# Scores in gate/up's array shape, from a zero-interleaved K ring, in a sliding-window attention and gated-MLP kernel

## The chip, the cores and the metric

The kernel runs on one core of one Trainium2 chip, as one program. The core has five engines with a queue each: TensorE (PE in the profile; its weight loads are listed as PEld) for matrix products, VectorE (DVE), ScalarE (ACT), GpSimd (POOL), and SyncE (SP), which issues the DMAs here. The engines meet at semaphores. PSUM, where PE writes, has eight banks of 512 float32 columns on 128 partitions; SBUF holds everything else. The metric is the device time of the program in microseconds (us). Three runs of the kernel before took 564.13 to 564.35 us, median 564.28.

## The reference

One sequence of 2048 tokens, 576 features. A layer norm without weights feeds two branches, and the output is x + attention x silu(MLP).

```python
xn = _layernorm(x, axis=-1)
# branch A: 32 heads of 18 features, causal window of 256 tokens
qkv = (xn @ wqkv)                               # 576 x 1728
scores = jnp.einsum("bhqd,bhkd->bhqk", q, k) * (18 ** -0.5)
mask = (idx[:, None] - idx[None, :] >= 0) & (idx[:, None] - idx[None, :] < 256)
p = _softmax(jnp.where(mask[None, None], scores, -1e9), axis=-1)
s = einsum("bhqk,bhkd->bhqd", p, v) -> (tokens, 576) @ wo
# branch B: 4608 hidden features
h = _sigmoid(xn @ w_gate) * (xn @ w_up)
g = _silu(h @ w_down)
return x + s * g
```

All inputs and the output are bfloat16.

## The kernel before

The tokens are cut into four chunks of 512 queries (`c` = 0 to 3). For each chunk the builder makes operations for the layer norm (L441 applies it), the Q, K and V projections (`project`, L491), attention, the output projection wo (L800), gate and up (`build_ffn`, L879), down (called f2, L1006) and the final product. The operations of all chunks go to a planner, `schedule`, a list scheduler with a cost for each operation (`mm_ns`, `act_ns`, `dve_ns`), a priority, and an extra cost `MODE_NS` of 94 ns where PE goes from one `mode` to another. It fixes the order of instructions on each of the five queues; on the chip each queue runs in that order and waits at semaphores. So attention of a chunk is woven into the gate/up matmuls of the same chunk.

The features are cut into 9 blocks of 64. Gate/up works in mode "r64": a matmul has 64 rows (half of the array) and 128 columns, and two of them, one on rows 0 to 63 and one on rows 64 to 127, run at the same time. A gate tile and an up tile have 9 such matmuls of 512 columns each; there are 36 hidden tiles to a chunk. ACT takes the gate's tanh (L893), DVE multiplies with up (L897, `hm`), and this frees the two banks. Gate/up uses banks 4 to 7. Projections and wo are r64 as well, with 288 columns. Down is mode "full" (128 x 128).

Heads stand in groups of four, `hg` = 0 to 7, each head in a strip of 32 partitions of `qkp`, the transposed Q and K (made by transposing DMAs from `pk`). Two head groups make a pair. A score unit (`build_unit`, mode "r32", L637) computes keys x queries in eight small tiles at once: four heads on four row strips of 18 rows, times two column halves of 64 keys, `low` the even key blocks of 64 and `up` the odd ones. Its pieces are runs of 1 to 6 query blocks of 64 columns. It fills all of banks 0 to 3, two exponentials of 128 x 1024 on ACT (L655) read them into `expr` (a ring of five), and DVE multiplies masks in (L673). The first chunk has two units per head group; the others have five per pair, as the blocks of the chunk before are needed as well: their K is kept by a tail copy on POOL (L684) which runs after the group's scores.

After a pair's units comes PV (`build_pv`, mode "c32", L707): eight tiles of 64 keys x 32 columns (18 of V and a one for the denominator). The even and the odd key blocks lie on different partition halves, so they end in different banks: two banks for each head group, four for the pair. In the chunks after the first, DVE transposes both (L726, L728) and adds them (L731); in the first chunk, ACT copies one (L740), DVE adds (L742) and transposes (L747). Then come reciprocal (L754), scaling (L758) and the transpose back (L764), and DMAs scatter the result to `oT` for wo. `SC_GATE` = 0 holds a chunk's scores back until the first gate/up step of that chunk has been planned. V is evicted by one ACT copy for each 128 tokens (L582), Q by DVE (L545) and K by ACT (L546).

At the start, ten matmuls on ones (L365) keep PE busy until the first normalized tokens arrive.

## Time and profile before

| | |
|---|---|
| median of three runs | 564.28 us |
| profiled execution | 564.0 us, of which the span of the profile 561.8 us |
| PE busy | 556.6 us |
| DVE / ACT / POOL busy | 305.3 / 279.3 / 29.6 us |
| gate/up windows of the four chunks | 21.85 to 103.79, 157.21 to 242.07, 295.31 to 380.42, 433.65 to 518.68 us |
| exponentials (L655) | 152 of 1.023 us |
| masks (L673) | 152, of 0.42 us where they have 512 elements |
| score matmuls (L637), PV matmuls (L707) | 1472, 1440 |

The span is the time from the first to the last instruction; what lies around it (2.2 us) belongs to the measured time. A group's line gives the line of the code, engine and operation, what is written from what with the shape, the number, then the busy time and the mean length of one in ns, and the idle time before them. The chain is followed back from the last instruction to what released it each time; in order of time, each of its pieces has start, length, and how many instructions the trace shows of it.

### The profile page before, as it was taken

What the parts mean: (1) busy time and instruction counts of PE and PEld (TensorE: products, weight loads), DVE (VectorE), ACT (ScalarE), POOL (GpSimd) and SP (SyncE); (2) the same over time, 40 slices, a digit from 0 to 9 for tenths busy, and PEclk for the clock granted to TensorE, in tenths of its full rate; (3) what the DMA queues carried; (4) which work ended last, traced back from release to release, by engine and by line L of the source; (5) the groups of instructions that cost most, each with busy time, mean ns of one, the idle gap of its engine ahead of it and who ended that gap; (6) DMA issues with size and microseconds to landing.
All of it is one profiled execution on the core that took longest, in us unless ns stands there. A gap on an engine that the chain in (4) does not pass through costs nothing.

```text
span 561.8 us, 17998 instructions
## 1 busy us (share of the span) xinstructions
PE 556.6 (99%) x7890; PEld 290.3 (52%) x7890; DVE 305.3 (54%) x656; ACT 279.3 (50%) x382; POOL 29.6 (5%) x55
## 2 busy tenths in 40 slices
PE   8999999999999999999999999999999999999997
PEld 5754444558544444456754444445664444444554
DVE  6135998722147886671215778766211586776312
ACT  7438777314065856811407576580230856856021
POOL 3000110100000110010000011001000000000100
PEclk9999999999999999999999999999999999999999
DMA  8999889837925766135992665604587355650010
GB/s 202 220 201 233 185 199 224 207 80 141 232 60 132 160 140 153 40 56 88 148 214 75 147 152 132 145 26 75 88 169 173 77 128 128 149 130 25 20 43 21
DMA packets 125898, 73.29 MB, mean 130 GB/s; under 512 B 54654, under 2 KB 125310, under 8 KB 125822
## 3 DMA queue, kind: packets, MB, share of 16 engines
q1 hardware_dynamic: 125822, 72.16, 60.3%
q8 instruction: 62, 1.02, 0.8%
q14 instruction: 14, 0.11, 0.1%
HBM read 55.48 MB, written 2.36 MB: 103 GB/s over the span
## 4 chain that ended last, share of the span: by engine, by line
PE 98%; DVE 1%; DMA 0%; issue 0%; ACT 0%
PE ps L879 51%; PE ps L1006 24%; PE ps L491 9%; PE ps L637 5%; PE ps L707 3%; PE ps L800 3%; PE ps L1037 2%; DMA xr<-in_A_x_dram 0%; DVE bnst L428 0%; DVE bnst L430 0%; DVE xnr L441 0%; PE ps L465 0%; DVE hT L897 0%; DVE op__63 L764 0%; DVE pk L728 0%; DVE mv L432 0%
## 5 line engine op out<-in xcount | busy, mean ns | idle before, releaser
L879 PE MATMUL ps<-xn,wgs 64*128 64x512 bf16 x2522 | 290.2, 377 | 0.0
L879 PEld LDWEIGHTS ps<-xn,wgs 64*128 64x128 bf16 x2522 | 117.5, 94 | 138.6 <-issue 10.2
L655 ACT ACTIVATE expr<-ps 128x1024 bf16<-128x1024 f32 x152 | 149.3, 1023 | 23.4 <-PE ps L637 23.4
L1006 PE MATMUL ps<-wd_sb,hT 128*128 128x512 bf16 (+1 forms) x1080 | 133.7, 286 | 0.0
L897 DVE SCALAR_TENSOR_TENSOR hT<-tring,ps 128x512 bf16<-128x512 bf16 x144 | 98.2, 682 | 49.2 <-ACT tring L893 25.9
L893 ACT ACTIVATE tring<-ps 128x512 bf16<-128x512 f32 x144 | 86.2, 599 | 77.5 <-PE ps L879 58.3
L1006 PEld LDWEIGHTS ps<-wd_sb,hT 128*128 128x128 bf16 x1080 | 68.1, 98 | 65.1 <-issue 1.4
L1068 ACT ACTIVATE thf<-ps 128x576 bf16<-128x576 f32 (+2 forms) x17 | 10.6, 623 | 133.2 <-PE ps L1006 125.6
L673 DVE TENSOR_TENSOR expr<-expr,m 128x512 bf16<-128x512 bf16 (+2 forms) x152 | 58.2, 412 | 33.1 <-ACT expr L655 32.0
L1070 DVE SCALAR_TENSOR_TENSOR thf<-thf,ps 128x576 bf16<-128x576 bf16 (+2 forms) x17 | 12.2, 719 | 107.4 <-ACT thf L1068 107.3
L491 PE MATMUL ps<-wqkv_sb,xn 64*128 64x288 bf16 x864 | 55.1, 283 | 0.1
L491 PEld LDWEIGHTS ps<-wqkv_sb,xn 64*128 64x128 bf16 x864 | 44.5, 94 | 8.6 <-issue 0.6
L637 PEld LDWEIGHTS ps<-qkp 18*64 18x64 bf16 x1472 | 16.4, 103 | 32.9 <-ACT expr L655 19.1
L637 PE MATMUL ps<-qkp 18*64 18x320 bf16 (+4 forms) x1472 | 32.4, 259 | 0.1
L684 POOL COPY qkp<-qkp 128x256 bf16<-128x256 bf16 x24 | 10.2, 423 | 292.2 <-PE ps L637 292.2
L764 DVE STREAM_TRANSPOSE op__63<-pk 128x512 bf16<-128x512 bf16 x32 | 22.5, 702 | 0.2
L707 PEld LDWEIGHTS ps<-expr,vau 64*32 64x32 bf16 x1440 | 17.9, 92 | 7.2 <-issue 5.5
L707 PE MATMUL ps<-expr,vau 64*32 64x320 bf16 (+5 forms) x1440 | 20.7, 253 | 0.0
L1072 DVE TENSOR_TENSOR thf<-thf,sat 128x576 bf16<-128x576 bf16 (+2 forms) x17 | 7.5, 440 | 23.1 <-ACT sat L824 22.8
L800 PE MATMUL ps<-wo_sb,oT 64*128 64x288 bf16 x288 | 18.8, 283 | 0.0
L800 PEld LDWEIGHTS ps<-wo_sb,oT 64*128 64x128 bf16 x288 | 14.5, 94 | 3.5 <-issue 0.5
L728 DVE STREAM_TRANSPOSE pk<-ps 128x512 f32<-128x512 f32 x24 | 16.1, 670 | 0.0
(62 smaller groups left out, 220.8 us busy)
## 6 DMA issues: line engine op xcount, KB each, us to landing
wgs<-in_B_w_gate_dram SPq DMA_DIRECT2D x47, 240.0 KB, 3.8
wgs<-in_B_w_up_dram SPq DMA_DIRECT2D x47, 240.0 KB, 4.9
wgs<-in_B_w_up_dram SPq DMA_DIRECT2D x47, 192.0 KB, 4.0
wgs<-in_B_w_gate_dram SPq DMA_DIRECT2D x47, 192.0 KB, 4.6
wd_sb<-in_B_w_down_dram SPq DMA_DIRECT2D x9, 576.0 KB, 6.7
xf<-in_A_x_dram SPq DMA_DIRECT2D x18, 144.0 KB, 2.4
out_dram<-xf SPq DMA_DIRECT2D x15, 144.0 KB, 2.0
xr<-in_A_x_dram SPq DMA_DIRECT2D x14, 144.0 KB, 4.0
```

The lines of the kernel that those rows point to most:

```text
L491: r = e.matmul(self.bank(ps, HV, hf), self.xn[r0:r0 + 64, k, i * P:(i + 1) * P], self.wqkv_sb[r0:r0 + 64, j, k, :], start=(k == 0), stop=( ...
L637: r = e.matmul(self.ps[64 * half:64 * half + 64, b:b + n * 64], self.qkp[r0:r0 + DH, hg, k0:k0 + 64], self.qkp[r0:r0 + DH, hg, q0 * 64:(q0 ...
L655: return e.activation(self.expr[:, es, 2 * pr:2 * pr + 2, :], src, ACTF.Exp, scale=SM_SCALE)
L673: return e.tensor_tensor(ap, ap, m, ALU.mult)
L707: r = e.matmul(self.ps[32 * j:32 * j + 32, b + q0 * 64:b + (q0 + n) * 64], vf[:, v0:v0 + 32], self.expr[p0:p0 + 64, es, j, pos * 64:(pos + ...
L728: t3 = self.rd("DVE", dve_ns(CH), lambda e, tg=tg, hg=hg: e.transpose(tg, self.bank(ps2[hg][1])), f"t3:{c}:{hg}", deps=[o, self.last_mul] ...
L764: t2 = self.op("DVE", dve_ns(CH), lambda e, on=on: e.transpose(self.op_[:, hg % NOT, :], on.rearrange("p g d -> p (g d)")), f"t2:{c}:{hg}" ...
L800: r = e.matmul(self.bank(ps2[w], HV, n), self.oT[r0:r0 + 64, kt, qi * P:(qi + 1) * P], self.wo_sb[r0:r0 + 64, kt, n * HV:(n + 1) * HV], st ...
L879: return e.matmul(self.bank((pg, pu)[gu][ft]), w, self.xn[r0:r0 + 64, i, :], start=first, stop=last, tile_position=(r0, 0))
L893: return e.activation(self.tring[:, st_, :], self.bank(ps), ACTF.Tanh, scale=0.5)
L897: return e.scalar_tensor_tensor(self.hT[:, ft, :], self.tring[:, st_, :], 1.0, self.bank(ps), ALU.add, ALU.mult)
L1006: r = e.matmul(self.ps[:, b + n0:b + n1], lhsT, self.wd_sb[:, q, fl, n0:n1], start=(ft == 0), stop=(ft == NFT - 1))
```

## The change

- **Heads.** Head h and head h + 16 stand on the two strips of 32 partitions of one row half. A head group is now two such pairs of heads, one on each row half.
- **K ring.** `build_kd` is new. For each head group DVE writes K of four key blocks into a ring `kd` of four slots: for each block of 64 keys, 128 columns, of which the first 64 have the second head's rows multiplied by zero and the last 64 the first head's rows (`hm` holds the zeros and ones). Two multiplies fill a slot; the first chunk takes two slots per head group, the others three.
- **Scores.** With these weights a matmul has 64 rows and 128 columns, mode "r64". The keys of the one head come out on partitions 0 to 63 and those of the other on 64 to 127, one bank per row half. A unit holds eight blocks of 64 queries (six in one of the first chunk's) in two banks, (0, 1) or (2, 3), and has one exponential. There are four units per head group in the first chunk and five in the others. `expr` becomes ten slots of half the size. The gate `SC_GATE` is gone.
- **V** is kept twice in the row sense: partitions 0 to 63 hold the values of heads 0 to 15, 64 to 127 those of heads 16 to 31, for each half of 64 tokens. Its eviction is four instructions, two on ACT and two on DVE.
- **PV** sums all key blocks of a head in one bank: two banks for a pair. One DVE transpose per head group follows, with no addition; the first chunk's path by copies is gone.
- **Around it.** The first chunk's Q and K evictions are split between ACT and DVE; wo's rows are loaded in the new order of heads, by four DMAs in place of two (the eight small ones stay); the tail copy waits for `kd` in place of the scores; the tanh buffer `thf` of the final product is taken from `expr`'s ring; the warm-up has 22 matmuls of 16 columns and nine of 512; the masks are built slightly differently.

```diff
-NEXP = 5
+NEXP = 10
...
-RTH = 2
 RREC = 2
+RKD = 4
+KD_NS = 180.0
+SC_PRIO = 1
+KD_PRIO = 0
...
-SC_GATE = 0
...
-WARM = 10
+WARM = 9
+TINY = 22
...
-        self.vau = sb("vau", [P, NVB, H + 1, DH + 1], bf16)
-        self.expr = sb("expr", [P, NEXP, 4, CH], bf16)
...
+        self.vau = sb("vau", [P, NVB, 2, H // 2 + 1, DH + 1], bf16)
+        self.kd = sb("kd", [P, RKD, 4, 2, 64], bf16)
+        self.expr = sb("expr", [P, NEXP, 2, CH], bf16)
...
-        self.thf = sb("thf", [P, RTH, D], bf16)
...
         def f(e):
-            for k in range(n):
-                r = e.matmul(self.bank(ps), self.hT[:, 0, 0:P], self.hT[:, 0, :], start=True, stop=True)
+            for w in [16] * TINY + [512] * n:
+                r = e.matmul(self.bank(ps, w), self.hT[:, 0, 0:P], self.hT[:, 0, 0:w], start=True, stop=True)
             return r
-        self.op_warm = self.pe(n * WARM_NS, f, name, deps=deps, prio=-9, psum=[ps])
+        self.op_warm = self.pe(n * WARM_NS + TINY * 30, f, name, deps=deps, prio=-9, psum=[ps])
...
+        rows = self.wo.rearrange("(s h t p) c -> p h t s c", s=2, h=2, t=2, p=KL)
         n = KL - (P - KL)
+        self.op_wo = []
+        for h, (r0, k) in enumerate(((0, KL), (KL, P - KL))):
+            for t in range(2):
+                self.op_wo.append(self.dma(self.wo_sb[r0:r0 + k, 2 * t:2 * t + 2, :], rows[0:k, h, t, :, :], 2 * k * D * 2,
+                                           f"wo{h}{t}", ("wo", h, t), deps=gate, prio=6))
...
+        ev = []
+        for k, (part, act) in enumerate(((slice(0, 1), 1), (slice(1, 2), 0)) if c == 0 else ((slice(0, 2), j),)):
+            n = D // 2 if c == 0 else D
+            ev.append(self.rd("ACT" if act else "DVE", act_ns(n) if act else dve_ns(n),
+                              lambda e, part=part, act=act: f_ev(e, part, act), f"qke:{c}:{i}:{j}:{k}", deps=deps, prio=1,
+                              psum=[ps]))
...
-        self.op_v[st] = self.rd("ACT", act_ns(D), f_ve, f"ve:{st}", deps=[o, self.op_vones], prio=1, psum=[ps])
+        self.op_v[st] = []
+        for s_, eng in ((0, "ACT"), (1, "DVE")):
+            for p in range(2):
+                def f_ve(e, s_=s_, p=p):
+                    src = self.bank(ps, HV, s_)[64 * p:64 * p + 64, :].rearrange("p (h d) -> p h d", d=DH)
+                    dst = self.vau[64 * s_:64 * s_ + 64, vs, p, 0:H // 2, 0:DH]
+                    return e.activation(dst, src, ACTF.Copy) if s_ == 0 else e.tensor_copy(dst, src)
+                self.op_v[st].append(self.rd(eng, (act_ns if s_ == 0 else dve_ns)(HV), f_ve, f"ve:{st}:{s_}{p}",
+                                             deps=[o, self.op_vones], prio=1, psum=[ps]))
...
     def attn_steps(self, c):
-        steps = []
+        if c == 0:
+            units = ([(0, 0, 5, 0), (5, 5, 3, 5)], [(1, 1, 5, 0), (6, 6, 2, 5), (7, 7, 1, 7)],
+                     [(2, 2, 5, 0), (3, 3, 3, 5)], [(3, 6, 2, 0), (4, 4, 4, 2)])
+        else:
+            units = ([(0, 0, 5, 0), (-2, 0, 3, 5)], [(1, 1, 5, 0), (-3, 0, 2, 5), (-4, 0, 1, 7)],
+                     [(-1, 0, 4, 0), (4, 4, 4, 4)], [(2, 2, 5, 0), (6, 6, 2, 5), (7, 7, 1, 7)],
+                     [(3, 3, 5, 0), (5, 5, 3, 5)])
+        masks = ([(0, 4, 0), (5, None, 0)], [(0, 4, 0), (5, 7, (0,))], [(0, 4, 0), (5, None, 0)], [(1, 2, 1)]) if c == 0 \
+            else ([(0, 4, 0), (7, None, 1)], [(0, 4, 0), (6, 7, (1,))], [(3, 4, 1)], [(0, 4, 0), (5, 7, (0,))],
+                  [(0, 4, 0), (5, None, 0)])
+        return list(zip(units, masks))
+
+    def build_attn(self, c):
+        self.masks, self.runs = {}, {}
+        steps = self.attn_steps(c)
         for a in range(0, NHG, 2):
...
+            for hg in (a, a + 1):
+                self.build_kd(c, hg)
+                for u, (pieces, masks) in enumerate(steps):
+                    self.build_unit(c, hg, u, pieces, masks)
+                for s_ in self.slots_kd.values():
+                    for o in self.op_sc[c][hg]:
+                        self.r_kd.release(s_, o)
+            self.build_pv(c, a)
+
+    def build_kd(self, c, hg):
+        self.slots_kd, self.ops_kd = {}, {}
+        for g in range(1 if c == 0 else 0, 3):
+            s_, ds = self.r_kd.take()
+            self.slots_kd[g] = s_
+            self.ops_kd[g] = []
+            deps = ds + self.op_hm + (([self.op_tail[hg]] if g == 0 else self.op_k[2 * g - 2:2 * g]))
+            for half in range(2):
+                def f_kd(e, g=g, s_=s_, half=half):
+                    if g == 0:
+                        src = self.qkp[:, hg, :].rearrange("p (j c) -> p j c", j=2)[:, :, CH:CH + P].rearrange(
+                            "p j (b c) -> p j b c", b=2)
+                        dst = self.kd[:, s_, :, half, :].rearrange("p (j b) c -> p j b c", j=2)
+                    else:
+                        src = self.qkp[:, hg, KO + (g - 1) * 256:KO + g * 256].rearrange("p (b c) -> p b c", b=4)
+                        dst = self.kd[:, s_, :, half, :]
+                    return e.tensor_scalar(dst, src, self.hm[:, half:half + 1], None, ALU.mult)
+                self.ops_kd[g].append(self.op("DVE", KD_NS, f_kd, f"kd:{c}:{hg}:{g}{half}", deps=deps, prio=KD_PRIO))
+        self.all_kd[hg] = [o for l in self.ops_kd.values() for o in l]
+
+    def build_unit(self, c, hg, u, pieces, masks):
         es, de = self.r_exp.take()
...
-        ps = Psum((0, 1, 2, 3))
...
+        ps = Psum((0, 1), (2, 3))
+        slots = dict(self.slots_kd)
+        pieces = sorted(pieces, key=lambda p: -p[2])
+        ncol = 64 * sum(p[2] for p in pieces)
 
         def f_sc(e):
-            for _, k in slots:
...
+            for kb, q0, n, pos in pieces:
+                for r in range(2):
+                    r0 = 64 * r
+                    w = self.kd[r0:r0 + 64, slots[(kb + 4) // 4], kb % 4, :, :].rearrange("p s c -> p (s c)")
+                    i = e.matmul(self.bank(ps, 512, r)[:, pos * 64:(pos + n) * 64], w,
+                                 self.qkp[r0:r0 + 64, hg, q0 * 64:(q0 + n) * 64], start=True, stop=True,
+                                 tile_position=(r0, 0))
+            return i
+        deps = list(de)
+        for kb, q0, n, pos in pieces:
+            deps += self.op_q[q0 // 2:(q0 + n + 1) // 2] + self.ops_kd[(kb + 4) // 4]
+            self.runs.setdefault(hg, []).append((kb, q0, n, es, pos))
+        o = self.pe(sum(mm_ns(64 * p[2]) for p in pieces), f_sc, f"sc:{c}:{hg}:{u}", deps=deps, prio=SC_PRIO, psum=[ps],
+                    mode="r64")
+        self.op_sc[c][hg].append(o)
...
+        ex = self.rd("ACT", act_ns(2 * ncol), f_ex, f"ex:{c}:{hg}:{u}", deps=[o], prio=1, psum=[ps])
+        out = [ex]
...
+            out.append(self.op("DVE", dve_ns(256 if pb is not None else 128, 2.0), f_mk, f"mk:{c}:{hg}:{u}:{pa}",
+                               deps=[ex] + self.op_mask, prio=1))
+        self.masks.setdefault(hg, []).extend(out)
...
-                    f"tail:{c}:{hg}", deps=self.op_sc[c][hg] + self.op_k[2:], prio=0)
-        ps2 = {hg: [Psum(*PVB) for _ in range(2)] for hg in pair}
...
+                    f"tail:{c}:{hg}", deps=self.all_kd[hg] + self.op_k[2:], prio=0)
+        ps2 = [Psum(*PVB) for _ in range(2)]
...
+        runs = {hg: sorted(self.runs[hg], key=lambda r: -r[2]) for hg in pair}
+        ncol = 64 * sum(r[2] for r in runs[a])
...
         def f_pv(e):
-            for hg in pair:
...
+            for m in range(len(runs[a])):
+                for cg in range(4):
+                    kb, q0, n, es, pos = runs[a + cg // 2][m]
+                    v0 = (2 * a + cg) * (DH + 1)
+                    for s_ in range(2):
+                        p0 = 64 * s_
+                        vf = self.vau[p0:p0 + 64, (kb0 + kb // 2) % NVB, kb % 2, :, :].rearrange("p h d -> p (h d)")
+                        r = e.matmul(self.bank(ps2[s_])[32 * cg:32 * cg + 32, q0 * 64:(q0 + n) * 64], vf[:, v0:v0 + 32],
+                                     self.expr[p0:p0 + 64, es, cg % 2, pos * 64:(pos + n) * 64], start=(m == 0),
+                                     stop=(m == len(runs[a]) - 1), tile_position=(p0, 32 * cg), skip_group_check=True)
             return r
         o = self.pe(ncol / 2.4 + 30, f_pv, f"pv:{c}:{a}", deps=self.masks[a] + self.masks[a + 1] + vdeps, prio=0,
-                    psum=ps2[a] + ps2[a + 1], mode="c32")
+                    psum=ps2, mode="c32")
...
-            t1 = self.rd("DVE", dve_ns(CH), lambda e, tf=tf, hg=hg: e.transpose(tf, self.bank(ps2[hg][0])),
...
-            t3 = self.rd("DVE", dve_ns(CH), lambda e, tg=tg, hg=hg: e.transpose(tg, self.bank(ps2[hg][1])),
...
-            ads = [self.op("DVE", dve_ns(16 * (DH + 1)), lambda e, tf=tf, tg=tg: e.tensor_tensor(tf, tf, tg, ALU.add),
...
+        for s_ in range(2):
+            t = a + s_
+            tf = self.pkf[:, 1 + s_, :, :].rearrange("p h d -> p (h d)")
+            tr = self.rd("DVE", dve_ns(CH), lambda e, tf=tf, s_=s_: e.transpose(tf, self.bank(ps2[s_])), f"t1:{c}:{t}",
+                         deps=[o, self.op_mul[c][t - 2] if t >= 2 else self.last_mul] + qk, prio=PV_PRIO[c > 0],
+                         psum=ps2[s_:s_ + 1])
+            self.after_pv(c, t, tf.rearrange("p (g d) -> p g d", d=32)[:, :, 0:DH + 1], tr)
...
-            if n0 == SC_GATE and c > 0:
-                for l in self.op_sc[c]:
-                    for u in l:
-                        u.odeps.append(o)
```

239 lines of the change are left out of this document (57 added, 182 removed).

## The prediction

> **What bounds the kernel now.** I read the page's first two parts first, then the chain that ended last, then the chain in order of time, and last the groups by shape and the stretches.
>
> ```profile
> PE 556.6 (99%) x7890; PEld 290.3 (52%) x7890; DVE 305.3 (54%) x656; ACT 279.3 (50%) x382; POOL 29.6 (5%) x55
> ...
> PEclk9999999999999999999999999999999999999999
> ...
> PE ps L879 51%; PE ps L1006 24%; PE ps L491 9%; PE ps L637 5%; PE ps L707 3%; PE ps L800 3%; PE ps L1037 2%; DMA xr<-in_A_x_dram 0%; DVE bnst L428 0%; DVE bnst L430 0%; DVE xnr L441 0%; PE ps L465 0%; DVE hT L897 0%; DVE op__63 L764 0%; DVE pk L728 0%; DVE mv L432 0%
> ```
> TensorE (PE) works without a break from about 6 us to the end, and the chain is PE for 98%. So an edit counts by the PE time that it takes or gives, and by any wait that it puts into PE's queue; VectorE (DVE) and ScalarE (ACT) count only if they hold PE up.
>
> The chain in order of time gives PE prices (start us, length us, line, matmuls seen):
>
> ```profile
> 21.85 21.37 PE ps L879 x198
> ...
> 54.78 0.36 PE ps L637 x16
> 55.14 2.48 PE ps L879 x22
> 57.62 1.04 PE ps L707 x53
> 58.67 2.48 PE ps L879 x22
> ...
> 128.44 2.20 PE ps L491 x36
> 130.64 2.21 PE ps L800 x36
> 132.85 6.62 PE ps L491 x108
> ```
> Long gate/up runs (L879) go at 21.37 us / 99 pairs = 0.2159 us; two matmuls of 64 rows run side by side. I use 0.2155, which fits the shorter runs better. A run of 22 between score units should take 11 x 0.2155 = 2.37 us and takes 2.48: coming back from another array shape costs 0.11 us. A score unit (L637) is 0.355 us itself, so it takes 0.467 us of PE. Between projection (L491) and wo (L800), both in gate/up's shape, nothing is lost: 2.20 us / 18 pairs = 0.1222 us for 288 columns (0.120 at 2.4 columns per ns), and 6.62/54 = 0.1226. The 0.11 us belongs to the change of shape.
>
> The second chunk's window closes the account: 157.21 to 242.07 us is 84.86; less 324 pairs x 0.2155 = 69.8, four PV groups of 1.28 + 0.11 and one entry of 0.11, leaves 9.4 us for 20 units, 0.47 each.
>
> ```profile
> 157.20:242.10 84.90, 84.90 (x1418) 38.55 (x1418) 61.34 (x135) 58.62 (x77) 5.86 (x12) 1.00 0.49 112
> ...
> 295.30:380.40 85.10, 84.96 (x1418) 38.53 (x1418) 61.31 (x135) 58.62 (x77) 5.86 (x12) 1.00 0.49 112
> ```
> Columns: stretch, length, then busy time of PE, weight load, DVE, ACT, GpSimd (POOL). DVE is at 72%, ACT at 69%.
>
> **The change, part by part.**
>
> *Scores removed.* 152 exponentials, two to a unit, make 76 units: 76 x 0.467 = 35.5 us of PE.
>
> *Scores added.* A unit now holds half as much: 64 x 128 weights, two row halves at once, where eight small tiles ran at once. There are 152 units. Chunks 2 to 4 have, per head group, 40 blocks of 64 queries: 2560/2.4 = 1067 ns, plus 12 pieces x 2.4 ns (the excess of 0.2155 over 512/2.4, and of 0.1222 over 0.120) = 1095. Two pieces are only 64 columns long. The nearest row is the transposes at the start, also 64 columns in 64 x 128 shape:
>
> ```profile
> 6.10 1.00 PE L465 MATMUL ps<-op__63,xnr 64*128 64x64 bf16 x36
> ```
> (1.00 - 0.19 for the latency of one)/35 is 23 ns each, about 50 ns a pair with the 0.66 us for 18, where the columns alone want 29. That adds 21 ns x 2: 1.137 us per group, x 24 = 27.3. The first chunk has 30 blocks, 9 pieces and one short piece: 843 ns x 8 = 6.7. Together 34.0 us; 32.8 if short pieces cost nothing. Pieces of 128 columns (53 ns) just cover the two weight loads of 46 to 50 ns.
>
> *PV (L707).* The same 1440 matmuls in the same eight tiles. In the first chunk 32 blocks a pair become 30: 4 x 2 x 27 ns = -0.2 us. Elsewhere nothing.
>
> *After PV.* In chunks 2 to 4, the second PSUM transposes (24 of 0.67) and 24 additions (0.45) go; in the first, eight ACT copies (0.6) and eight additions (0.69). PV takes two banks instead of four, and a score unit two of four, so scores run on while PV is evicted. None of it is on the chain but for one spot at 340.7, where PE waited for DVE's transposes; the third and fourth windows are 0.2 us longer than the second. I take -0.2 us, between 0 and -0.4. What is late there next is the tile's own multiply (L897), which the gate/up banks wait for.
>
> *The K ring (kd).* 6 DVE multiplies per head group in chunks 2 to 4, 4 in the first: 176 of 128 x 256. Nearest rows:
>
> ```profile
> L445 DVE COPY xnr<-xnr 128x64 bf16<-128x64 bf16 x16 | 2.9, 180 | 0.3
> ...
> L673 DVE TENSOR_TENSOR expr<-expr,m 64x256 bf16<-64x256 bf16 x8 | 2.3, 290 | 0.3
> ```
> So 0.18 to 0.29 us each; I take 0.22 (one input as in the copy, the multiply's length). Masks: per chunk 40 of 512 elements (0.76 us for two back to back, 0.38 each) become 56 of 256 and 16 of 128, about 0.25 and 0.18 in a row: 15.2 to 16.9 us. DVE in the second chunk's window: 61.3 + 1.7 + 48 x 0.22 - 8 x (0.63 + 0.38) = 65.5 of 84 us, 78%. ACT keeps its 40 exponentials. So as a sum it is hidden under PE at nothing. If that cover goes, it costs by its waits: scores wait for kd; kd of the second and third K group must wait for the last score of the head group before, since four slots serve groups of three. Behind a waiting score in PE's queue stand gate/up matmuls; behind a waiting kd on DVE stand masks and L897, and gate/up waits for that. Bounds: 0, as before's scores waited for exponentials without a PE gap (the next line: the weight loads' idle time, matmuls ran on under it), to one uncovered DVE instruction of 0.6 us at each of 24 head groups of chunks 2 to 4, 14 us. I take 0, nearest to that row, since the order puts gate/up in front of the scores.
>
> ```profile
> PEld ps L637 <- ACT expr L655: 19.1, 45, 0.4
> ```
> *V and first-chunk evictions.* 16 ACT copies of 576 columns (0.65) become 32 on ACT and 32 on DVE, 288 columns on 64 partitions: 0.41 and 0.45, between the rows for 128 and 512 columns. From 121.5 to 139.5 us DVE is busy 6.0 and ACT 7.5 us of 18; they get 3.6 and 0.7 more. A bank pair is held some 0.4 us longer, with four pairs and a projection each 1.1 us. Nothing; the same for the first chunk's Q and K split over both engines (PE has no gap from 10.8 to 21.9 us).
>
> *Queues.* Two more wo loads on SP's queue, at 0.6 us of issue each, delay the down-weight loads behind them by 1.2 us, 20 us before their use. POOL's tail copies now wait for kd, before the scores, so rstd behind them on POOL is freed sooner. The scores are no longer held behind the chunk's first gate/up step; first scores 2 us sooner, with nothing to gain on PE. The tanh buffer becomes slots of the exponentials' ring: 4 of 10 stay taken until the finals at about 159 us, when some eight units later need them. All nothing.
>
> *Start.* One cold matmul of 512 (4.45 us less the last one's 0.61 is nine steps of 0.427) goes, 22 of 16 columns come: 13 ns each by columns at the cold pace, up to 0.15 as a weight load there lasts, so -0.1 to +2.9 us; near the short transposes, doubled for the cold clock, some 0.03 to 0.05. PE has work at once at 6.1, so I take +0.3.
>
> Sum: -35.5 + 34.0 - 0.2 - 0.2 + 0.3 = **-1.6 us**. The profiled execution took 564.0 us (span 561.8 and 2.2 around it), so 562.4 there; the median of the runs, 564.28, lies 0.28 above it: **562.7 us**. What a measurement of this kernel can tell from no change is about 0.2%, 1.1 us, so the forecast lies just beyond it.
>
> **The rivals.**
>
> *Slower: kd paces PE.* Place: the head-group boundaries in chunks 2 to 4. The chain there is last score, two kd multiplies, next score, and with attention running more tightly DVE gets near full: per head group 2.1 of masks, 1.3 of kd, 0.6 + 0.2 + 0.3 + 0.6 for transposes and scaling is 5.1 us, and L897 0.26 of the time, so some 7 us against 7.1 that a group takes now. For it, the second pair of the first chunk (DVE 13.4 of 14.0 us):
>
> ```profile
> 58.70:72.70 14.00, 14.00 (x200) 5.93 (x206) 13.43 (x37) 11.88 (x16) 2.14 (x4) 1.00 0.83 192
> ```
> Against it: PE has no gap even there, and a chunk leaves 84/8 = 10.5 us a group. At 0.6 us for a third of 24 boundaries it gives 562.7 + 4.8 = 567.5. It decides from 1.6/24 = 0.07 us a boundary.
>
> *The shape costs nothing, the hand-over does.* If the 0.11 us is paid wherever a group of other matmuls begins, because PE waits at its semaphore, each of 152 units still pays: +16.7, 579. Against it: projection and wo alternate free of it.
>
> *The start eats it.* The page shows full clock throughout, but the warm-up's 0.427 us a matmul is half pace, for 4.3 us. If the tiny matmuls do not count as work and the clock opens one such stretch later, 4.3 us at half pace lose 2.1: 564.8, within 0.2%. The Trainium skill, "TensorE: Matmul & The Clock Gate", Part 1, says that a monitor of PE's activity opens the clock after about 3.4 us of sustained work, in windows that run free of the kernel; by its figure the loss would be 1.7 us. The trace agrees with a stretch of this size; how tiny matmuls are counted it doesn't show.
>
> *More is won.* Short pieces free (-1.2), both late windows cured (another -0.2), the start neutral (-0.3): 561.0. For it: the weight loads' queue idles beside gate/up and could hide a short piece's loads.
>
> **How the numbers follow.** Forecast (562 to 563.3) 0.42; more won 0.13; the start or as much lost in small waits 0.21; kd paces PE 0.18; hand-over 0.06. Faster by over 0.2%: the forecast less its last tenth of a microsecond, and more won, 0.53; within: 0.22; slower: the last two and a late start, 0.25. The range reaches down to 560.9 and up to 567.2, leaving out the hand-over, half of kd's worst and the best of the gain.
>
> **What would show it.** Scores as 720 matmuls, with 22 gate/up matmuls between two units at 2.37 us, not 2.48: shape confirmed. A unit at 0.22 us in the chain: sizes confirmed; those with a short piece 0.02 longer. DVE at about 78% in the windows, kd near 0.22. Wrong if the chain shows DVE L897 or kd pieces at head-group boundaries, if PE's busy share falls under 98%, or if the first projection starts later than 7.4 us.

## The result

The changed kernel takes 565.23 us (median of 22 runs, 564.59 to 566.01), the kernel before beside it 564.22 (563.99 to 564.67): a ratio of 1.0017, 95% interval 1.0010 to 1.0023. It is 1.0 us slower, where 1.6 us faster was forecast. The profiled execution took 564.74 us, half a microsecond under the median, with a span of 562.9 against 561.8. What lies around the span is about 1.8 us in the runs of the changed kernel and of all its variants, and 2.2 in those of the kernel before; the forecast carried the 2.2 over. So by the span the change costs some 1.4 us in the median, and the profile shows 1.1 of it. Why the part around the span got shorter is not known.

From the page of the changed kernel, engines, granted clock and the chain by engine and line (gate/up is now L857, scores L655, PV L711, down L980, kd L639, masks L683, the tile's own multiply L875):

```profile
PE 553.6 (98%) x7136; PEld 308.3 (55%) x7159; DVE 320.4 (57%) x927; ACT 274.4 (49%) x394; POOL 29.0 (5%) x56
...
PEclk9999999999999999999999999999999999999999
...
PE 94%; DVE 3%; DMA 1%; issue 1%; SPq 0%; POOL 0%; ACT 0%; DVEq 0%; POOLq 0%
PE ps L857 48%; PE ps L980 23%; PE ps L492 8%; PE ps L655 6%; PE ps L711 4%; PE ps L778 3%; PE ps L1011 2%; DMA qkp<-pk 1%; DVE hT L875 1%; DVE expr L683 1%; DVE kd L639 0%; DVE bnst L429 0%; SPq L230 0%; DVE bnst L431 0%; DVE xnr L442 0%
```

PE's busy time is 3.0 us less than before (553.6 against 556.6), and yet the span is 1.1 us longer: the profile shows PE idle for 9.3 us in place of 5.2. Some 2 of the 9.3 are not idle time: the trace has 1129 matmuls of down where the kernel before has 1152, and the missing ones leave gaps of 1.95 us. The chain says whom PE waits for: its own share fell from 98% to 94%, and DVE and the transposing DMAs came in.

The score units themselves do what the change says. PE in order of time in the second chunk (start us, length us, then the work; a length includes the time to the modelled end of the last matmul, so starts are compared):

```profile
159.22 1.68 PE L857 MATMUL ps<-xn,wgs 64*128 64x512 bf16 x14
160.73 0.39 PE L655 MATMUL ps<-qkp,kd 64*128 64x320 bf16 x6
160.95 1.03 PE L857 MATMUL ps<-xn,wgs 64*128 64x512 bf16 x8
161.81 0.38 PE L655 MATMUL ps<-qkp,kd 64*128 64x320 bf16 x4
162.03 1.24 PE L857 MATMUL ps<-xn,wgs 64*128 64x512 bf16 x10
```

Fourteen gate/up matmuls take 160.73 - 159.22 = 1.51 us, 0.2157 a pair: nothing is lost on the way from one kind to the other. A unit takes 0.22 us, and the unit with a 64-column piece (six matmuls) no more than the one without (four).

I added up, over the trace, the time from the first matmul of each run of one kind to the first of the next run:

| | before | changed |
|---|---|---|
| scores | 27.3 us in 76 runs | 33.8 in 145 (0.7 of it at two units ahead of down) |
| gate/up | 290.2 us in 94 runs | 285.3 in 154 |

At 0.2155 us a pair gate/up needs 279.3 us. Before, the rest was 10.9 us, or 0.115 for each of 94 runs. In the changed kernel only the 16 returns from PV and the four entries from down and projections should cost that, 2.2 us, which makes 281.5. The two score units ahead of down seem to take 0.55 us each, because down's first records are missing and the time until the next one seen is counted with them; without that the scores take 33.1. So scores and shape together should give 33.1 + 281.5 - 27.3 - 290.2 = -2.9 us, more than forecast. Of gate/up time 3.8 us are left over; 0.9 of that is down's missing records at the ends of the four windows, and some 3 us are waits.

Where the waits are, three places of the changed kernel show. First DVE in order of time between 200 and 204 us, and below it POOL and PE from the same stretch, PE with its wait for DVE:

```profile
200.32 0.67 DVE L875 SCALAR_TENSOR_TENSOR hT<-tring,ps 128x512 bf16<-128x512 bf16 x1
200.92 1.47 DVE L639 TENSOR_SCALAR kd<-qkp,hm 128x256 bf16<-128x256 bf16 x6
202.31 0.68 DVE L683 TENSOR_TENSOR expr<-expr,m 128x256 bf16<-128x256 bf16 x3
202.91 0.68 DVE L875 SCALAR_TENSOR_TENSOR hT<-tring,ps 128x512 bf16<-128x512 bf16 x1
203.51 0.21 DVE L683 TENSOR_TENSOR expr<-expr,m 128x128 bf16<-128x128 bf16 x1
```

```profile
201.84 0.47 POOL L693 COPY qkp<-qkp 128x256 bf16<-128x256 bf16 x1 [5.11 <-DVE kd L639]
...
203.78 1.38 PE L711 MATMUL ps<-expr,vau 64*32 64x320 bf16 x96 [0.22 <-DVE expr L683]
```

DVE is full, with six kd multiplies in one go, and PV waits for its last mask. The six take (202.31 - 200.92)/6 = 0.232 us each, but not evenly: the six start 0.196 us apart, and the sixth, beside which POOL makes its tail copy (second fence), takes 0.49 and is followed after 0.41. In the whole trace eight of the 176 multiplies take 0.43 to 0.49 us, all beside a tail copy; the others take 0.28. On the average of the later chunks the next instruction starts 0.208 us after a multiply; the planner reckons with 0.18.

Second, the change of the second chunk to the third, PE's queue around the start of down's last blocks:

```profile
278.19 0.40 PE L655 MATMUL ps<-qkp,kd 64*128 64x320 bf16 x4 [0.66 <-DMA qkp<-pk]
278.51 2.56 PEld L980 LDWEIGHTS ps<-wd_sb,hT 128*128 128x128 bf16 x22 [0.21 <-issue]
...
278.74 2.61 PE L980 MATMUL ps<-wd_sb,hT 128*128 128x64 bf16 x20 [0.16 <-DVE vau L592]
```

With the old hold gone, the planner put one score unit ahead of down. It waits 0.66 us for the DMA transposes of Q and K, and down, which needs none of them, stands behind it in PE's queue. (The gap of 0.16 ahead of down is where its first records are missing.)

Third, the start, the mask copy on DVE and the first transposes on PE:

```profile
2.37 0.91 DVE L350 COPY m<-m 64x192 bf16<-64x192 bf16 x1 [0.41 <-POOL m L347]
...
3.31 0.46 DVE L429 BATCH_NORM_STATS2 bnst<-xr 128x6 f32<-128x288 bf16 x1
...
6.38 1.00 PE L466 MATMUL ps<-op__63,xnr 64*128 64x64 bf16 x36 [0.83 <-DVE mv L433]
```

The copy of the masks on DVE now stands ahead of the layer norm (before, DVE copied them after 8 us), and the layer norm begins behind it, at 3.31 in place of 3.03; PE's first transposes come at 6.38 in place of 6.10.

### The profile page after: what moved, and what is told of

Its sections match the earlier page's. It is cut to its first block, busy times and chain, and to the rows that moved or that the text cites. A ratio compares the mean times of both kernels' runs of the same rounds, so it can differ in the third digit from the quotient of the medians.

```text
span 562.9 us, 16766 instructions
## 1 busy us (share of the span) xinstructions
PE 553.6 (98%) x7136; PEld 308.3 (55%) x7159; DVE 320.4 (57%) x927; ACT 274.4 (49%) x394; POOL 29.0 (5%) x56
## 4 chain that ended last, share of the span: by engine, by line
PE 94%; DVE 3%; DMA 1%; issue 1%; SPq 0%; POOL 0%; ACT 0%; DVEq 0%; POOLq 0%
PE ps L857 48%; PE ps L980 23%; PE ps L492 8%; PE ps L655 6%; PE ps L711 4%; PE ps L778 3%; PE ps L1011 2%; DMA qkp<-pk 1%; DVE hT L875 1%; DVE expr L683 1%; DVE kd L639 0%; DVE bnst L429 0%; SPq L230 0%; DVE bnst L431 0%; DVE xnr L442 0%
## 5 line engine op out<-in xcount | busy, mean ns | idle before, releaser
L857 PE MATMUL ps<-xn,wgs 64*128 64x512 bf16 x2522 | 299.8, 376 | 0.1
L857 PEld LDWEIGHTS ps<-xn,wgs 64*128 64x128 bf16 x2522 | 122.4, 94 | 114.6 <-issue 1.3
L669 ACT ACTIVATE expr<-ps 128x1024 bf16<-128x1024 f32 (+1 forms) x152 | 148.9, 1030 | 20.4 <-PE ps L655 20.4
L875 DVE SCALAR_TENSOR_TENSOR hT<-tring,ps 128x512 bf16<-128x512 bf16 x144 | 98.2, 682 | 75.4 <-PE ps L857 55.9
L980 PE MATMUL ps<-wd_sb,hT 128*128 128x64 bf16 (+1 forms) x1057 | 131.1, 284 | 1.9 <-issue 1.0
L980 PEld LDWEIGHTS ps<-wd_sb,hT 128*128 128x128 bf16 x1080 | 68.1, 98 | 65.6 <-issue 2.1
L1042 ACT ACTIVATE expr<-ps 128x576 bf16<-128x576 f32 (+2 forms) x17 | 10.6, 623 | 126.5 <-PE ps L980 118.9
L683 DVE TENSOR_TENSOR expr<-expr,m 128x256 bf16<-128x256 bf16 (+1 forms) x272 | 59.9, 267 | 6.9 <-ACT expr L669 6.1
L1044 DVE SCALAR_TENSOR_TENSOR expr<-expr,ps 128x576 bf16<-128x576 bf16 (+2 forms) x17 | 12.2, 719 | 86.4 <-ACT expr L1042 86.4
L655 PE MATMUL ps<-qkp,kd 64*128 64x320 bf16 (+3 forms) x720 | 57.1, 252 | 0.7 <-DMA qkp<-pk 0.7
L655 PEld LDWEIGHTS ps<-qkp,kd 64*128 64x128 bf16 x720 | 32.7, 94 | 35.7 <-ACT expr L669 5.5
L639 DVE TENSOR_SCALAR kd<-qkp,hm 128x256 bf16<-128x256 bf16 x176 | 40.6, 287 | 12.1 <-DMA qkp<-pk 8.7
L711 PEld LDWEIGHTS ps<-expr,vau 64*32 64x32 bf16 x1440 | 18.4, 92 | 8.2 <-issue 3.4
L711 PE MATMUL ps<-expr,vau 64*32 64x320 bf16 (+4 forms) x1440 | 20.7, 254 | 0.5 <-DVE expr L683 0.4
L592 DVE CAST vau<-ps 64x288 bf16<-64x288 f32 x32 | 14.6, 458 | 8.2 <-PE ps L492 7.6
```

The lines of the kernel that those rows point to most:

```text
L639: return e.tensor_scalar(dst, src, self.hm[:, half:half + 1], None, ALU.mult)
L655: i = e.matmul(self.bank(ps, 512, r)[:, pos * 64:(pos + n) * 64], w, self.qkp[r0:r0 + 64, hg, q0 * 64:(q0 + n) * 64], start=True, stop=Tru ...
L669: return e.activation(self.expr[:, es, :, 0:ncol], src, ACTF.Exp, scale=SM_SCALE)
L683: return e.tensor_tensor(ap, ap, m, ALU.mult)
L711: r = e.matmul(self.bank(ps2[s_])[32 * cg:32 * cg + 32, q0 * 64:(q0 + n) * 64], vf[:, v0:v0 + 32], self.expr[p0:p0 + 64, es, cg % 2, pos * ...
L857: return e.matmul(self.bank((pg, pu)[gu][ft]), w, self.xn[r0:r0 + 64, i, :], start=first, stop=last, tile_position=(r0, 0))
```

## The experiments

| kernel | edit to the changed kernel | median us | before beside it | ratio (95%) |
|---|---|---|---|---|
| e1_gate2 | scores of the third chunk held behind down | 564.84 | 564.16 | 1.0009 (1.0001 to 1.0018) |
| e2_cols64 | scores in 64-column tiles | 594.9 | 564.16 | 1.0543 (1.0529 to 1.0558) |
| e6_masks | masks on one column of 64 | 563.75 | 564.16 | 0.9990 (0.9981 to 0.9999) |
| e5_warm | old warm-up | 564.63 (one run) | | |
| f6_gm | scores held, mask copy later | 564.91 | 564.30 | 1.0008 (0.9999 to 1.0016) |
| f1_gkm | the same, and kd planned at 240 ns | 563.20 | 564.30 | 0.9975 (0.9964 to 0.9987) |
| f2_gkmr | the same, and slots freed sooner | 563.24 | 564.30 | 0.9979 (0.9970 to 0.9988) |
| f3_pool | as f1, a third of kd's later groups on POOL | 563.79 | 564.30 | 0.9989 (0.9980 to 0.9997) |
| e3_kdns | kd planned at 240 ns, nothing else | 564.26 | 564.35 | 1.0000 (0.9991 to 1.0009) |
| g1_split | as f1, 240 ns for the later chunks only | 562.44 | 564.35 | 0.9968 (0.9956 to 0.9979) |
| g2_splitr | as g1, and slots freed sooner | 562.51 | 564.35 | 0.9965 (0.9953 to 0.9978) |
| g4_nocopy | as g1, mask copy early | 562.82 | 564.37 | 0.9975 (0.9964 to 0.9986) |

### Is it the shape? (e2_cols64)

```diff
-                    w = self.kd[r0:r0 + 64, slots[(kb + 4) // 4], kb % 4, :, :].rearrange("p s c -> p (s c)")
-                    i = e.matmul(self.bank(ps, 512, r)[:, pos * 64:(pos + n) * 64], w,
...
-                                 tile_position=(r0, 0))
+                    for s_ in range(2):
+                        i = e.matmul(self.bank(ps, 512, r)[64 * s_:64 * s_ + 64, pos * 64:(pos + n) * 64],
+                                     self.kd[r0:r0 + 64, slots[(kb + 4) // 4], kb % 4, s_, :],
...
+                                     tile_position=(r0, 64 * s_))
```

> The changed kernel in the same planned order, with each score matmul cut into two of 64 columns on the two column halves of the array, so that only the array shape of the scores changes (64 x 64 in place of 64 x 128); the computation is the same. Theory: the price of before, 0.11 us for each return to gate/up, belongs to the change of shape, and some 145 groups of scores pay it again, plus a fill of up to 0.14: 565.2 + 16 to + 37, that is 581 to 602. Rival: the hand-over between groups does not depend on the shape, as the changed kernel's 0.22 us units have hidden it in another way: within 2 us of 565.2.

594.9 us, 29.7 over the changed kernel, inside the expectation. The order on every queue is the same, and only the score matmuls are cut in two. PE's chain in order of time in that kernel (start, length, work):

```profile
168.81 0.34 PE ps L655 x8
169.16 1.19 PE ps L858 x10
170.34 0.34 PE ps L655 x8
170.68 0.97 PE ps L858 x8
```

Ten gate/up matmuls (1.078 us by pairs) take 1.19, so the 0.11 us of before is back, and the unit takes 0.34 in place of 0.22. Some 145 groups at 0.23 would be 33 us; 29.7 came. The longer unit does not come from its doubled number of matmuls: in the trace, units of eight and of twelve matmuls take 0.345 and 0.348 us (medians). So the price belongs to the shape, both parts of it. That settles the rival of the hand-over.

### Is it VectorE? (e6_masks, f3_pool)

```diff
+                ap, m = ap[..., 0:1], m[..., 0:1]
                 return e.tensor_tensor(ap, ap, m, ALU.mult)
```

> The changed kernel in the same planned order, with each mask multiply working on one column of each 64 only (so most of the causal and window masking is left out): 272 multiplies get some 0.1 us shorter, 25 us of DVE in all. Theory: gate/up windows of the changed kernel lose some 2.6 us to PE waits because VectorE, with 176 K-ring multiplies of 0.24 us where the planner counts 0.18, falls behind its plan; with the shorter masks those waits go: 562.8 to 563.8. Rival: the lost time in the windows does not come from VectorE: 564.9 to 565.4.

563.75 us: 1.5 less, in the expected range, with the same order on every queue. In its profile the wait of PV at 203 us is gone, and DVE's load from 157 to 247 us falls from 67.0 to 60.3 us. With the order unchanged, this shows that VectorE costs PE time in the windows. But it is not full there: 67 of 90 us. The next runs ask whether it lacks time or its plan is wrong.

> As the second kernel in the list, with the first K group of each head group (the keys of the chunk before, 48 of the 176 multiplies) made by GpSimd in place of VectorE, and wo kept off gate/up's banks. It takes 3.8 us of VectorE's work out of each of the later windows and changes nothing else. Theory that VectorE's load costs PE the time: 562.6 to 563.2. Rival: GpSimd is slower at it (its copy of the same size takes 0.42 us) and holds up the layer norm's POOL step and the tail copies behind it: 564 or more.

```diff
-                self.ops_kd[g].append(self.op("DVE", KD_NS, f_kd,
+                self.ops_kd[g].append(self.op("POOL" if g == 0 else "DVE", 450 if g == 0 else KD_NS, f_kd,
```

563.79 us, between what was expected and its rival's 564, and 0.6 more than f1_gkm with all of kd on VectorE. The groups of kd in that kernel:

```profile
L639 POOL TENSOR_SCALAR kd<-qkp,hm 128x256 bf16<-128x256 bf16 x48 | 46.5, 980 | 188.1 <-PE ps L655 188.1
...
L639 DVE TENSOR_SCALAR kd<-qkp,hm 128x256 bf16<-128x256 bf16 x128 | 36.3, 336 | 21.7 <-DMA qkp<-pk 19.1 <-PE ps L655 2.5
```

GpSimd takes 0.98 us for one, where the planner of this run was told 0.45, and VectorE's own got longer (0.336 us against 0.287): 49 of its 128 take 0.30 to 0.50, all beside work on GpSimd. So VectorE's load from 157 to 247 us is 64.9 us against 66.8 in f1_gkm, less by 2 and not by the 3.8 that were expected. This run carries a wrong price of its own; it shows that the move is no gain, not what a well planned one would give.

### Is it the planner's price? (f6_gm, f1_gkm, e3_kdns)

```diff
-KD_NS = 180.0
+KD_NS = 240.0
```

This is all of e3_kdns. f6_gm and f1_gkm have this hold on the scores and the later mask copy; f6_gm also has wo's bank rule (shown with g1_split), without which the planner finds no order at 180 ns, and at 240 ns the rule changes nothing in any queue:

```diff
-                    mode="r64")
+                    mode="r64", odeps=[self.f2_ops[(QPC - 1, NWD - 1)]] if c in (1, 2, 3) else [])
...
-                           prio=2)]
+                           prio=30)]
```

> The changed kernel with the scores of all later chunks held until the last down step of the chunk before, with the mask copy at the start moved behind the layer norm, and with wo kept off gate/up's banks where its eviction waits for gate/up's end (the plan finds no order otherwise). Theory of two small losses outside the gate/up windows: the waits for the K transposes before down go in both chunks (0.7 to 1.0 us of the median) and the start comes 0.28 us sooner: 563.9 to 564.3. Rival: the transposes' wait only shows up at another place: 565.0 or more.

> As the kernel before this one in the list (hold of all later chunks, mask copy behind the layer norm; wo's banks as in the changed kernel), and the planner counts 240 ns for a K-ring multiply in place of 180, near the 235 to 245 ns at which they follow each other in the trace. Theory: VectorE falls behind the plan because that price is too low; with the right price, PE's waits in the gate/up windows shrink by a half of the 1.5 us which the short masks won: 563.1 to 563.6. Rival: VectorE is short of time whatever the plan believes: no better than 563.9 to 564.3.

> The changed kernel with one number altered: the planner counts 240 ns for a K-ring multiply in place of 180. Theory: the gate/up windows' PE waits come from a plan that believes VectorE faster than it is; alone, without the hold on the scores, the right price takes 1.0 to 1.7 us off, as it did beside the hold: 563.5 to 564.3. Rival: it was the two together, or the luck of one order: 564.8 to 565.4.

f6_gm: 564.91, outside the theory's range and next to the rival's 565.0; the 0.3 us under the changed kernel are within the noise (the intervals overlap). f1_gkm: 563.20, so one number is worth 1.7 us there. e3_kdns: 564.26, 1.0 us better than the changed kernel by the same number. Both lie in the theory's range. The trace puts the gain in the later windows: from the first gate/up or score matmul to down, with wo's 4.4 us inside, they take 89.77, 89.91 and 89.27 us in f6_gm and 88.96, 89.04 and 88.96 in f1_gkm (all records of down are present in both). Without wo, f1's 84.5 to 84.6 us compare with 84.9 to 85.1 in the kernel before. VectorE does the same work in both; only the order differs. The other kernels agree with this: the windows of the second and third chunk take 88.9 to 89.3 us in the six kernels planned at 240 ns there (e3, f1, f2, g1, g2, g4; f3_pool with its wrong price for GpSimd apart), and 89.6 to 90.1 in the four planned at 180 (the changed kernel, e1, e5, f6), missing records included. In the fourth chunk, where VectorE has 61 us of work in place of 66 to 67, they hardly differ.

That 240 is the right price is not shown. It lies above the 0.208 us of the trace, no other price was run, and a new price also makes a new order. By the planner's own reckoning, which is arithmetic and not a run, those two windows last 88.8 us in f6_gm and 88.4 in f1_gkm: of the 0.8 to 0.9 us by which each gets shorter on the chip, about half is a shorter plan, and the other half is that the chip keeps closer to it.

The hold did less than expected in f6_gm; its order loses elsewhere what it wins there: its second of these windows, 89.91, is 0.3 us longer than the changed kernel's 89.63 (in which a missing record adds some 0.2, while one score unit of 0.22 stands outside, ahead of down).

### The hold on the scores (e1_gate2)

```diff
-                    mode="r64")
+                    mode="r64", odeps=[self.f2_ops[(QPC - 1, NWD - 1)]] if c in (2,) else [])
```

> The changed kernel, with the scores of the third chunk held until the last down step of the second. Theory: without the old gate, one score unit stands in PE's queue ahead of down's last blocks and waits there for the K transposes (0.66 us of idle PE in the profile, and more in runs where those DMAs land later); with the hold the time falls by 0.8 to 1.3 us, to 563.9 to 564.4, and its spread gets narrower. Rival: the wait only moves, since PE has to pass the same work later, and the time stays within 0.3 us of 565.2.

564.84 us, 0.4 less: between the two, and within the noise, as the intervals of both ratios overlap. In its profile the wait at 278 us is gone, but the third chunk's window takes 90.14 us against 89.63; 0.22 of that is the unit which now stands inside, so the new order loses 0.3 elsewhere. A second reason why the median fell by less than 0.66 us is in the profile of e5_warm, whose planned order is that of the changed kernel. There the unit at 278 us does not wait, but the one ahead of the fourth chunk does:

```profile
416.87 0.39 PE L655 MATMUL ps<-qkp,kd 64*128 64x320 bf16 x4 [0.65 <-DMA qkp<-pk]
```

So the wait comes now at one chunk, now at the other, and a hold at one of them takes away a part. Beside the price of 240, hold and mask copy together are worth 564.26 - 563.20 = 1.1 us (e3_kdns against f1_gkm, from two series on two chips).

### The start (e5_warm, g4_nocopy)

```diff
-WARM = 9
-TINY = 22
+WARM = 10
+TINY = 0
```

> The changed kernel with the old warm-up, ten matmuls of 512 columns and no short ones. The prediction's step: the 22 short matmuls delay the start by 0.3 us, so the first transposes come at 6.1 us again, not at 6.4. Rival: the late start comes from the mask copy on VectorE which now stands ahead of the layer norm, so the transposes stay at 6.3 to 6.4 us.

In this one run the first transposes stay at 6.37 us, so the short warm-up matmuls are not what delays them. In f6_gm, with the copy behind the layer norm, they come at 6.10. Whether that reaches the end:

> As the fastest kernel so far (562.44), but with the mask copy of the start back in front of the layer norm, as the changed kernel has it. If the copy's 0.28 us at the first transposes reaches the end, 562.7; if the projections behind them wait for the weights anyway (they began at 10.8 us with either place of the copy), 562.3 to 562.6.

562.82 us (562.39 to 563.73) against g1_split's 562.44 (562.10 to 562.93). The ratios' intervals overlap, 0.9964 to 0.9986 and 0.9956 to 0.9979, so a gain of 0.3 us fits and is not shown. From 15.3 us PE stood still for 0.7 us for the projection weights in g1_split's profile, which can hide the start's gain in one run or another; and in the profiles of the changed kernel and of f6_gm gate/up begins at the same time, 21.81 and 21.85 us.

### The ring (f2_gkmr, g2_splitr) and the best version (g1_split)

```diff
-                for s_ in self.slots_kd.values():
-                    for o in self.op_sc[c][hg]:
-                        self.r_kd.release(s_, o)
+                for g, s_ in self.slots_kd.items():
+                    for (pieces, _), o in zip(steps, self.op_sc[c][hg]):
+                        if any((p[0] + 4) // 4 == g for p in pieces):
+                            self.r_kd.release(s_, o)
```

> As the kernel before this one in the list, with wo kept off gate/up's banks as in the first, and with each K-ring slot freed by the scores that read it, in place of all scores of its head group. Theory that kd's wait for the last score of the head group before paces the scores (the prediction's slower rival): another 0.5 us or more, 562.5 to 563.1. Rival: the ring is not what is waited for: within 0.3 us of the kernel before this one.

> As the kernel before this one in the list, and each K-ring slot freed by the scores that read it. Theory that the ring is not what is waited for: within 0.3 us of that kernel. Rival, the ring paces the scores: 0.5 us or more below it.

563.24 against 563.20, and 562.51 against 562.44: the wait of kd for the scores of the head group before, which was the place of the prediction's slower rival, costs nothing that can be measured.

The first window was longer in f1_gkm (82.28 us) than in f6_gm (81.44), with a wait of PE for the tile's multiply at 97 us, so g1_split keeps 180 ns there. Its other edits are those of f6_gm, with wo's bank rule:

```diff
-                self.ops_kd[g].append(self.op("DVE", KD_NS, f_kd,
+                self.ops_kd[g].append(self.op("DVE", KD_NS if c == 0 else 240.0, f_kd,
...
-            ps2 = [Psum((4, 5), (6, 7), (0, 1), (2, 3)) for _ in pair]
             slots = [self.r_s.take() for _ in pair]
+            ps2 = [Psum((0, 1), (2, 3)) if ss == self.sx else Psum((4, 5), (6, 7), (0, 1), (2, 3)) for ss, _ in slots]
```

> The hold on the scores of the later chunks, the mask copy behind the layer norm, wo kept off gate/up's banks where its eviction waits for gate/up's end, and 240 ns for the K-ring multiply in the planner for the later chunks only; the first keeps 180, since its window was longer with 240 (82.28 us against 81.44). Theory: the windows' savings add up, 0.5 us better than with 240 everywhere (563.2): 562.4 to 563.0. Rival: the first window's difference is not the price's but the startup's, which varies with the weights' arrival: 563.0 to 563.4.

562.44 us, ratio 0.9968 (0.9956 to 0.9979): 1.9 us faster than the kernel before and 2.8 faster than the change as it was made. The time is what the theory of added savings gave, and its first window is 81.68 us. But the price is not what decides that window: f3_pool, planned at 240 ns there too, has 81.63, and g2_splitr, planned at 180, has 82.36 and is no slower (562.51). So what the first window adds to the time is open. Busy times of it and of the kernel before in two stretches (columns as before: length, PE, weight load, DVE, ACT, POOL):

```profile
157.00:247.00 90.00, 89.84 (x1306) 46.99 (x1304) 66.80 (x206) 59.00 (x80) 6.80 (x12) 1.00 0.48 109
297.00:386.00 89.00, 88.84 (x1294) 46.58 (x1292) 67.04 (x207) 58.59 (x80) 6.95 (x13) 1.00 0.49 110
```
```profile
157.00:247.00 90.00, 90.00 (x1459) 41.16 (x1458) 66.21 (x147) 58.62 (x77) 5.86 (x12) 1.00 0.50 111
297.00:386.00 89.00, 88.86 (x1449) 40.66 (x1446) 66.00 (x148) 57.97 (x76) 5.86 (x12) 1.00 0.51 114
```

VectorE has nearly the same load, 67 against 66 us, in some 60 instructions more. The two PE gaps of 0.16 us in g1_split are places where the first records of down are missing. The changed kernel in the same stretches, with its waits:

```profile
157.00:247.00 90.00, 89.56 (x1297) 48.10 (x1294) 66.97 (x206) 59.42 (x80) 6.96 (x12) 1.00 0.49 109
297.00:386.00 89.00, 88.56 (x1286) 47.00 (x1284) 66.32 (x204) 57.95 (x79) 6.81 (x12) 1.00 0.50 110
```

The lengths of the windows tell more than the busy time: from the first gate/up or score matmul to down, the three later ones take 89.18, 89.18 and 89.20 us in g1_split, and 90.00, 89.63 and 89.50 in the changed kernel.

## Why the prediction was wrong, point by point

- **Scores removed and added: right, with the size off.** Forecast -35.5 + 34.0 = -1.5 us, measured -2.9 by the sums of runs: some -36.0 + 33.1. The term that was mis-sized is the short piece: 21 ns each was taken from transposes that follow one another with nothing but short matmuls, and beside pieces of 320 and 128 columns it costs nothing (four and six matmuls both take 0.22 us). A unit is 0.2176 us on average (33.07/152 in g1_split) where 0.224 was taken. PV's -0.2 did not come: 19.6 us before, 19.7 after.
- **The shape's price: right.** 0.11 us on each return, gone in the changed kernel, back in e2_cols64. "The shape costs nothing, the hand-over does" fell.
- **"I take 0" for the K ring: the step that failed.** The duration was near (0.22 taken; VectorE is busy for 40.6 us with 176 of them, 0.231 each, since one lasts 0.28 and the next begins 0.196 after it), and the load too (78% forecast; 67.0 of 90 us, 74%, seen). The 0 stood for the waits that kd puts into PE's queue, and it was no 0: with the same order and shorter masks on VectorE the time falls by 1.5 us (e6_masks), and with orders planned at 240 ns by 1.0 (e3_kdns) and 1.7 (f1_gkm against f6_gm). The prediction gave as its reason that the order puts gate/up in front of the scores. But the queues are laid out beforehand, with 0.18 for a multiply after which the next instruction starts 0.208 us later on average: over 48 multiplies a window VectorE falls behind that order by some 1.3 us, an estimate from these two figures, at places where PV and the gate/up banks wait for it. The diff shows the 180 (`KD_NS`), and it was not compared with the 0.22. How much of the loss is this price, and how much an order that happened to be long, stays open.
- **"kd paces PE", the slower rival: right on the engine, wrong on the mechanism.** The chain holds DVE pieces of kd, masks and L875, which the prediction had set as a sign of being wrong; the ring's wait is not their cause (f2_gkmr, g2_splitr).
- **"All nothing" for the hold taken off the scores: failed.** The prediction saw only that the first scores come 2 us sooner. It did not ask what stands behind a score unit that goes further ahead: down, which is held up when the transposes land late. 0.66 us in the profile; hold and mask copy together are worth 1.1 us of the median, beside the price of 240.
- **Start: +0.3 was right in size by luck, and wrong in cause.** 0.28 us at the first transposes (and the first projection at 7.46 us, past the 7.4 set as a sign), from the mask copy and not from the short matmuls (e5_warm). How much of it arrives at the end stays open: gate/up's first matmul starts at 21.81 us, against 21.67 before.
- **"The start eats it": fell.** In the trace of the changed kernel the 22 short matmuls follow each other at 27 ns, then those of 512 columns at 427, and the last two steps are 314 and 216 ns: the clock opens some 3.3 us after the first of them (an estimate from these steps). This agrees with the Trainium skill, "TensorE: Matmul & The Clock Gate", Part 1, which gives about 3.4 us and says that the windows run free of the kernel. The time varies: of the twelve profiles with the short matmuls four open between 3.1 and 3.6 us, and eight are at half pace for 3.97 us at least; the two with the old warm-up are so for 3.81 at least. So how short matmuls are counted stays open, but it costs little: where the first 36 transposes still run slowly (e2_cols64, f3_pool, g2_splitr) they take 0.90 us from the first start to the last in place of 0.81, so that 0.1 us is lost there and not 2.1.
- **After PV, -0.2: not seen as such.** The changed kernel's later windows have other waits in its place; in g1_split they are 0.02 us apart, so the old difference between the windows is gone there.
- **The sum.** -2.9 for scores and shape; some 3 for gate/up's waits, of which 1.0 to 1.7 go with the planner's price; 0.7 for the transposes; 0.1 to 0.3 for the start: about +1, near what the spans have (562.9 against 561.8). With edits against the three losses g1_split comes out at 562.44, and the forecast said 562.7. That they lie so near is in part luck: 0.4 of g1_split's 1.9 us lie around the span, where no term of the forecast stood. By the median of its spans (560.65 against 562.15) it gains 1.5 us, and the rest of the 2.9 was not traced further; 0.9 of it is gate/up time (283.3 us, less 281.5 and 0.9 for down's missing records).

## What to carry to other kernels

Where the order of work is written out beforehand by a planner with a price for each instruction, a new instruction's price belongs beside the time from one to the next in the trace, and other prices are worth a run: one number, 180 or 240 ns for 48 short instructions in a window of some 85 us, was worth 1.0 to 1.7 us here, a third to more than half of what the change had won. An edit that lifts a hold is to be followed down the queue: it is free only if the instruction that moves ahead is never the one that waits. And small tiles that fill the array are not cheaper than large ones half full of zeros, if each return from another shape costs 0.11 us and the visit 0.12 more.

## What the runs showed of the hardware that I had not expected

- Going into 64 x 64 tiles and back costs a unit 0.23 us (0.34 + 0.11 against 0.22), as much again as the unit itself.
- A 64-column matmul of 64 x 128 costs no more than its columns when longer pieces stand around it, while a row of nothing but short transposes goes at 23 to 25 ns for each instruction (prediction's row, L465).
- GpSimd takes 0.98 us for the multiply of 128 x 256 bfloat16 that VectorE does in 0.287, and while GpSimd made a part of them VectorE's rose to 0.336 on average. In the changed kernel VectorE's take 0.28 us alone, and 0.43 to 0.49 where GpSimd's tail copy runs beside them (eight of 176).
- The wait for the transposing DMAs stands at another chunk in another profile of the same planned order (0.66 us at 278 us in the changed kernel, 0.65 at 417 in e5_warm, 0.14 and 0.10 at both in e6_masks), so one profile does not say how often it comes.
